# Loading the two halves of the first piece of x through ScalarE's queue in a gated attention and GLU kernel

## The chip, the cores and the metric

The kernel runs on one core of one Trainium2 chip. The metric is the time of one execution in device microseconds; the figure given for a kernel is the median of its runs. Below, TensorE (PE) multiplies matrices, PEld is its loading of the stationary operand, VectorE (DVE), ScalarE (ACT) and GpSimd (POOL) work on elements, and SyncE (SP) issues transfers. ScalarE can issue transfers too, from its own queue. A transfer is issued by an engine's queue and carried out by the core's 16 DMA engines; a semaphore tells when it has landed.

## The reference

The input x has 2048 rows of 512. The reference mixes two branches with a gate per row:

```
g = sigmoid(sum(x * gate_w))                      # one number per row
a = attention(x @ wqkv) @ wo                      # 32 heads of 16, each row sees the 256 rows up to itself
b = (sigmoid(x @ w_gate) * (x @ w_up)) @ w_down   # 1376 hidden columns
out = g * a + (1 - g) * b
```

All of it is float32.

## The kernel before

Every product of two float32 operands is made from three matmuls. An operand is split into a rounded high part, made by ScalarE's cast, and the rest, made by VectorE's subtraction (the function `split`, lines 75 and 76); the products high x high, high x low and low x high are added in PSUM. x is kept transposed in SBUF as `xh` and `xl`: 128 partitions, four pieces of the contraction (`d`, 0 to 3) and 2048 columns, which are the rows of x. It arrives in four chunks of 512 columns (`c`), each of four pieces `d` of 128 x 512.

The program runs in stages: the value projection of the first four blocks of 128 rows (tile `vps`, line 440), the query and key projections (`pj`), the rest of the value blocks, the windowed attention interleaved with the gate and up projections (`gu`), and last the down projection and the output projection (`pd`, `pa`). The order on TensorE, ScalarE, VectorE and SyncE is the order in which the program is written; a planner places only GpSimd's instructions. Waits on semaphores follow from the tiles that an instruction reads and writes. Eight semaphores serve the transfers in turn, so a transfer waits until the one eight before it has landed.

The change touches the first loads of the first stage. Before them line 185 issues 14 matmuls on zeros (`warm`). Then, for each `d`, the loop in lines 189 to 195 loads the value weights `wv` of that piece (256 KB), splits them into `wvh` and `wvl`, loads the piece of x of chunk 0 (256 KB) and splits it. For `d = 0` the piece of x is loaded and split in two halves of 256 columns (128 KB each), so that the matmuls of the first two blocks can begin with the first half. All these transfers are issued by SyncE. `xraw` and `wvraw`, into which they go, are parts of the tile `V`, which the profile therefore names as their destination; `wvh` goes by the name `w`. After the loop come the loads of the query and key weights (`wqraw`, line 144) and of the chunks 1 to 3 of x (line 168).

TensorE takes `d = 0` in two parts, the first two blocks for all three products and then the other two; from `d = 1` on it takes four blocks for each product:

```
for w, bb in (
    [(w, (2 * h, 2 * h + 1)) for h in range(2) for w in range(3)] if d == 0
    else [(w, range(4)) for w in range(3)] if d < ND - 1 else [(None, range(4))]
):
```

So `d = 0` has 12 matmuls, and those of its first half need `wv` piece 0 and the first half of x.

Of the kernel before, what the change touches and what calls it, by code (L numbers as in the profile page):

```python
# [22 lines left out]
CH = 512  # L23
# [33 lines left out]
def gated_mix_kernel(  # L57
# [11 lines left out]
    nc = tc.nc  # L69
# [4 lines left out]
    def split(hi, lo, src):  # L74
        nc.scalar.copy(hi, src)  # L75
        nc.vector.tensor_tensor(lo, src, hi.bitcast(F32), op=ALU.subtract)
# [52 lines left out]
    with ExitStack() as actx:  # L129
# [30 lines left out]
        xraw = Vf[:, NB * VROW - 2 * ND * CH:].rearrange("p (c d t) -> p c d t", c=2, d=ND)  # L160
# [22 lines left out]
        def idle_mm(n):  # L183
            for _ in range(n):
                mm(warm_ps[:, 0:2 * P], warm[:, 0:P], warm[:, 0:2 * P], start=True, stop=True)

        idle_mm(14)

        for d in range(ND):
            nc.sync.dma_start(wvraw[:, d], wv_v[:, d])  # L190
            split(wvh[:, d], wvl[:, d], wvraw[:, d])
            for h in range(2) if d == 0 else (None,):
                ts = slice(0, CH) if h is None else slice(h * CH // 2, (h + 1) * CH // 2)
                nc.sync.dma_start(xraw[:, 0, d, ts], xT[0, d][:, ts])
                split(xh[:, d, ts], xl[:, d, ts], xraw[:, 0, d, ts])
        raw_q = [load_wqk(g) for g in range(2)]
        load_x(1)
# [294 lines left out]
        def gu_mm(f, c, w, k, half=None, second=False):  # L492
            if (f, c, w) not in gp:
                gp[f, c, w] = ps.tile([P, CH], F32, tag="misc", name=f"gu{f}_{c}_{w}", bufs=3)
            group_mm(gp[f, c, w], gv[:, 0, w], gv[:, 1, w], c, k, half, second)
# [90 lines left out]
        def proj_slot(s, k, half):  # L586
            g, c = divmod(s, NC)
            d, w = divmod(k, 2) if k < 2 * ND else (k - 2 * ND, 2)
            r = slice(64 * half, 64 * half + 64)
            mm(pair_of_banks(f"ph{s}")[half], wq[g][int(w == 2)][r, d], (xl if w == 1 else xh)[r, d, c * CH:(c + 1) * CH],  # L590
               start=k == 0, stop=k == 3 * ND - 1)

        def proj_sum(s):
            lower, upper = halves.pop(f"ph{s}")
            t = cpool.tile([P, CH], F32, tag="sp", name=f"psum{s}", bufs=4)
            nc.scalar.copy(t, lower)
            pj[s] = t
            behind.append(lambda: nc.vector.tensor_tensor(t, upper, t, op=ALU.add))
            soon.append(lambda: proj_post(s))
# [6 lines left out]
                lambda k, h=None, x=False, a=(f, c, w): gu_mm(*a, k, h, x),  # L606
# [159 lines left out]
        for u in range(N):  # L766
# [34 lines left out]
            for s4 in proj_at.get(u, ()):  # L801
                if u < LAG:
                    first.insert(0, (
                        lambda k, h, s4=s4: proj_slot(s4, k, h), lambda s4=s4: proj_sum(s4)))
# [113 lines left out]
        for n, (c, f) in enumerate(steps):  # L918
# [34 lines left out]
            for t in range(4):  # L953
                ts = slice(t * P, (t + 1) * P)
# [72 lines left out]
```

## Time and profile before

| what | value |
|---|---|
| time, median of 3 runs | 738.04 us (737.7 to 738.16) |
| time of the profiled execution | 737.77 us |
| its span, first to last instruction | 736.1 us |
| TensorE busy | 730.0 us, 99% of the span |
| VectorE, ScalarE, GpSimd busy | 507.1, 430.4, 170.7 us |
| granted TensorE clock | 1.000 |
| moved by the DMA engines | 103.65 MB, mean 141 GB/s |

In a row of the view in order of time the first number is the start in us from the beginning of the span, the second the length; then come engine, line, operation, destination and source with their shapes and the count. Brackets hold the idle time ahead of it and what ended it. SPq is the queue in which SP issues transfers; the length there is that of the issue, not of the transfer. In the view of stretches each engine has its busy time and the number of its instructions, and the last three columns are the granted clock of TensorE, the busy share of the 16 DMA engines and the rate in GB/s. In the chain of work that ended last each row is start, length and what held the chain.

### The profile page before, as it was taken

How to read it: one execution, taken by the hardware profiler on the slowest of the kernel's cores; microseconds unless marked ns; L12 is line 12 of the kernel's file. 1: busy time of each engine (PE TensorE's matmuls, PEld its weight loads, DVE VectorE, ACT ScalarE, POOL GpSimd, SP SyncE). 2: the span in 40 equal slices, each digit the busy share in tenths (PEclk: the TensorE clock that was granted, in tenths of full speed). 3: DMA queues.
4: the chain of work that ended last, by engine and by line, in shares of the span. 5: the costliest groups of instructions: out<-in, count | busy, mean ns of one | idle time of the engine just before them, and what ended most of it. 6: DMA issues, size and time to landing. Idle time of an engine off the chain costs nothing.

```text
span 736.1 us, 17727 instructions
## 1 busy us (share of the span) xinstructions
PE 730.0 (99%) x6298; PEld 578.3 (79%) x6298; DVE 507.1 (69%) x1519; ACT 430.4 (58%) x922; POOL 170.7 (23%) x256
## 2 busy tenths in 40 slices
PE   9999999999999999999999999999999999999997
PEld 7888777887777878778777777778887888787886
DVE  5378867667776776776777677678846877658481
ACT  6423666576666666756757667676566654534341
POOL 5200333233233232323323323323341000000000
PEclk9999999999999999999999999999999999999999
DMA  8441334534445353452534524544477867878431
GB/s 300 108 116 43 102 106 120 152 88 127 129 116 142 86 153 109 123 156 59 165 106 107 152 76 128 160 135 152 154 233 190 281 173 175 224 172 252 131 74 57
DMA packets 94464, 103.65 MB, mean 141 GB/s; under 512 B 44942, under 2 KB 57486, under 8 KB 94376
## 3 DMA queue, kind: packets, MB, share of 16 engines
q1 hardware_dynamic: 94376, 102.53, 50.0%
q8 instruction: 49, 0.80, 0.5%
q14 instruction: 39, 0.32, 0.1%
HBM read 45.32 MB, written 31.99 MB: 105 GB/s over the span
## 4 chain that ended last, share of the span: by engine, by line
PE 97%; DVE 1%; DMA 1%; issue 1%; ACT 0%; SPq 0%; DVEq 0%
PE gu L245 28%; PE pv L394 12%; PE pj L245 11%; PE s L315 7%; PE st L361 5%; PE tp L539 5%; PE pd L79 5%; PE pd L81 5%; PE pd L80 5%; PE vh L576 3%; PE pa L79 2%; PE pa L80 2%; PE pa L81 2%; PE vps L440 1%; DVE junk L321 1%; DMA V<-in_wv_dram 1%
## 5 line engine op out<-in xcount | busy, mean ns | idle before, releaser
L321 DVE CUSTOM_DVE_ANT_0 junk<-s,mask 128x384 f32<-128x384 f32 (+2 forms) x512 | 271.6, 530 | 123.4 <-PE s L315 57.3
L366 ACT ACTIVATE pt<-st 128x384 f32<-128x384 f32 (+2 forms) x512 | 241.1, 475 | 166.0 <-PE st L361 66.6
L245 PE MATMUL gu<-xh,w 64*128 64x512 f32 x1152 | 271.1, 393 | 0.0
L245 PE MATMUL gu<-xl,w 64*128 64x512 f32 x576 | 183.0, 392 | 0.0
L371 POOL TENSOR_SCALAR_AFFINE_SELECT pt<-pt 128x512 f32<-128x512 f32 x128 | 86.5, 675 | 373.2 <-ACT pt L366 369.6
L361 PE MATMUL st<-ring 64*128 64x384 f32 (+2 forms) x536 | 168.1, 331 | 0.0
L315 PE MATMUL s<-ring 64*128 64x384 f32 (+2 forms) x536 | 166.7, 329 | 0.7 <-DVE mx L321 0.7
L245 PEld LDWEIGHTS gu<-xh,w 64*128 64x128 f32 x1152 | 150.9, 185 | 13.7
L315 PEld LDWEIGHTS s<-ring 64*128 64x128 f32 x536 | 95.3, 184 | 39.8 <-DVE nm L332 8.1
L361 PEld LDWEIGHTS st<-ring 64*128 64x128 f32 x536 | 96.3, 184 | 10.3 <-issue 2.7
L394 PE MATMUL pv<-pt,V 128*32 128x384 f32 (+2 forms) x1408 | 91.0, 388 | 0.0
L245 PEld LDWEIGHTS gu<-xl,w 64*128 64x128 f32 x576 | 87.7, 185 | 4.0
L245 PE MATMUL pj<-xl,wqh 64*128 64x512 f32 (+1 forms) x228 | 80.0, 392 | 0.0
L245 PE MATMUL pj<-xh,wqh 64*128 64x512 f32 (+1 forms) x228 | 79.8, 392 | 0.0
L376 POOL TENSOR_SCALAR_AFFINE_SELECT pt<-pt 128x512 f32<-128x512 f32 x112 | 74.8, 668 | 0.0
L245 PE MATMUL pj<-xh,wql 64*128 64x512 f32 (+1 forms) x228 | 69.8, 391 | 0.0
L394 PEld LDWEIGHTS pv<-pt,V 128*32 128x32 f32 x1408 | 37.2, 109 | 35.1 <-issue 28.8
L79 PE MATMUL pd<-ring,hb 128*128 128x512 f32 x160 | 63.1, 395 | 0.0
L81 PE MATMUL pd<-ring,hb 128*128 128x512 f32 x160 | 62.8, 393 | 0.0
L80 PE MATMUL pd<-ring,hb 128*128 128x512 f32 x160 | 62.1, 388 | 0.0
L75 ACT CAST hb<-V 128x512 fp32r<-128x512 f32 x40 | 24.9, 622 | 61.7 <-DVE V L730 47.7
L245 PEld LDWEIGHTS pj<-xh,wql 64*128 64x128 f32 (+1 forms) x228 | 41.2, 185 | 3.1
(129 smaller groups left out, 1133.1 us busy)
## 6 DMA issues: line engine op xcount, KB each, us to landing
gu_scratch<-sp SPq DMA_DIRECT2D x72, 256.0 KB
V<-gu_scratch SPq DMA_DIRECT2D x36, 512.0 KB
ring<-sh SPq DMA_DIRECT2D x128, 128.0 KB
ring<-sl SPq DMA_DIRECT2D x64, 128.0 KB
guraw<-in_wgu_dram SPq DMA_DIRECT2D x18, 256.0 KB
oT_scratch<-ob SPq DMA_DIRECT2D x128, 32.0 KB
xl<-oT_scratch SPq DMA_DIRECT2D x16, 256.0 KB
out_dram<-spare SPq DMA_DIRECT2D x16, 256.0 KB
```

What stands on the lines that cost most here:

```text
L79: mm(ps, lh, rh, start=first, stop=False)
L80: mm(ps, lh, rl, start=False, stop=False)
L81: mm(ps, ll, rh, start=False, stop=last)
L245: mm(pt, (wl if w == 2 else wh)[r, d], (xl if w == 1 else xh)[r, d, c * CH:(c + 1) * CH], start=k == 0 and not second, stop=k == 3 * ND - ...
L315: mm(pt[:, (k - k0) * P:(e - k0) * P], lhsT, blk(g, k, hh, 1, e - k), start=k == k0, stop=e == i + 1, skip_group_check=True,)
L321: nc.vector.tensor_tensor_reduce(junk[:, 0:n], pt[:, 0:n], mask[:, 3 * P - n:], scale=1.0, scalar=NEG, op0=ALU.add, op1=ALU.max, accum_out ...
L361: mm(pt[:, (q - j) * P:(e - j) * P], lhsT, blk(g, q, hh, 0, e - q), start=q == j, stop=e == last, skip_group_check=True,)
L366: nc.scalar.activation(pts[u][:, hh, 0:n], pt[:, 0:n], AF.Exp, scale=SCALE)
L371: nc.gpsimd.affine_select(p[:, :, 0:P], p[:, :, 0:P], pattern=[[0, HG], [1, P]], compare_op=ALU.is_ge, fill=0.0, base=0, channel_multiplie ...
L376: nc.gpsimd.affine_select(p[:, :, 2 * P:], p[:, :, 2 * P:], pattern=[[0, HG], [-1, P]], compare_op=ALU.is_gt, fill=0.0, base=0, channel_mu ...
L394: mm(pv[32 * hh:32 * hh + 32, (q % 4) * P:(q % 4 + e - q) * P], V[:, j, h * VW:h * VW + 32], p[:, hh, (q - j) * P:(e - j) * P], start=Fals ...
L539: mm(tp[b][:, 0:TW], (xl if w == 1 else xh)[r, d, b * P:(b + 1) * P], tw[d][int(w == 2)][r, 0:TW], start=k == 0 and not second, stop=k == ...
```

## The change

The two halves of the piece `d = 0` of x are issued by ScalarE, ahead of the loop. In the loop SyncE issues the four weight pieces and the pieces 1 to 3 of x. The splits, and the order of all that is computed, stay as they are.

```diff
         idle_mm(14)
 
+        pieces0 = [slice(h * CH // 2, (h + 1) * CH // 2) for h in range(2)]
+        for ts in pieces0:
+            nc.scalar.dma_start(xraw[:, 0, 0, ts], xT[0, 0][:, ts])
         for d in range(ND):
             nc.sync.dma_start(wvraw[:, d], wv_v[:, d])
             split(wvh[:, d], wvl[:, d], wvraw[:, d])
-            for h in range(2) if d == 0 else (None,):
-                ts = slice(0, CH) if h is None else slice(h * CH // 2, (h + 1) * CH // 2)
-                nc.sync.dma_start(xraw[:, 0, d, ts], xT[0, d][:, ts])
+            if d > 0:
+                nc.sync.dma_start(xraw[:, 0, d], xT[0, d])
+            for ts in pieces0 if d == 0 else (slice(0, CH),):
                 split(xh[:, d, ts], xl[:, d, ts], xraw[:, 0, d, ts])
         raw_q = [load_wqk(g) for g in range(2)]
```

## The prediction

> **What bounds the kernel now.** I read the page first: the share of each engine and the chain that ended last.
>
> ```profile
> span 736.1 us, 17727 instructions
> ...
> PE 730.0 (99%) x6298; PEld 578.3 (79%) x6298; DVE 507.1 (69%) x1519; ACT 430.4 (58%) x922; POOL 170.7 (23%) x256
> ...
> PE 97%; DVE 1%; DMA 1%; issue 1%; ACT 0%; SPq 0%; DVEq 0%
> ```
>
> TensorE is busy for 730.0 of 736.1 us and holds 97% of the chain. So this kernel is a single row of matmuls, and a change in how the first operands are loaded can pay only by what it moves at the start of that row. Everything behind the point from which TensorE no longer waits moves along by the same amount. The second view is therefore the chain in the first 9 us.
>
> ```profile
> 0.80 0.40 SPq L190
> ...
> 1.26 0.41 SPq L194
> ...
> 1.72 0.42 SPq L194
> ...
> 2.19 4.34 DMA V<-in_wv_dram
> ...
> 6.55 0.62 ACT w L75
> ...
> 7.19 0.63 ACT xh L75
> ...
> 7.86 1.19 PE vps L440 x4
> ```
>
> SP issues the first weight piece (I call it w0), the two halves of the first piece of x (x0a, x0b) and then the second weight piece (w1). w1 is on its way from 2.19 to 6.53 us. ScalarE rounds it, then rounds x1, and TensorE begins the second quarter of the contraction (d = 1) at 7.86. Three issues of SP stand ahead of w1 on this chain, and the change takes two of them away. The third view is ScalarE in order of time, to see when each operand is there.
>
> ```profile
> 0.80 1.28 ACT L75 ACT_TABLE_LOAD   x1 [0.80 <-PEq L1014]
> 3.54 0.62 ACT L75 CAST w<-V 128x512 fp32r<-128x512 f32 x1 [1.47 <-DMA V<-in_wv_dram]
> 4.07 0.40 ACT L75 CAST xh<-V 128x256 fp32r<-128x256 f32 x1
> 5.35 0.41 ACT L75 CAST xh<-V 128x256 fp32r<-128x256 f32 x1 [0.88 <-DMA V<-in_xT_dram]
> 6.55 0.62 ACT L75 CAST w<-V 128x512 fp32r<-128x512 f32 x1 [0.79 <-DMA V<-in_wv_dram]
> 7.19 0.62 ACT L75 CAST xh<-V 128x512 fp32r<-128x512 f32 x1
> ...
> 8.52 0.62 ACT L75 CAST xh<-V 128x512 fp32r<-128x512 f32 x1
> ```
>
> A cast begins 0.02 us after the transfer that it waited for (w1: 6.53 in the chain, 6.55 here). So w0 lands at 3.52, x0a by 4.07 (no wait ahead of its cast), x0b at 5.33, w1 at 6.53, x1 by 7.19. The fourth view is TensorE's weight loads, one for each matmul, in which a stop is seen more exactly than in the matmuls, whose ends are modelled.
>
> ```profile
> 4.52 0.49 PEld L440 LDWEIGHTS vps<-w,xh 128*128 128x128 f32 x2 [0.21 <-ACT xh L75]
> ...
> 6.90 0.42 PEld L440 LDWEIGHTS vps<-w,xl 128*128 128x128 f32 x2
> 7.86 0.76 PEld L440 LDWEIGHTS vps<-w,xh 128*128 128x128 f32 x4 [0.55 <-ACT xh L75]
> 8.67 0.87 PEld L440 LDWEIGHTS vps<-wvl,xh 128*128 128x128 f32 x4
> 9.59 0.89 PEld L440 LDWEIGHTS vps<-w,xl 128*128 128x128 f32 x4
> ```
>
> From 8.67 to 9.59 four loads take 0.92 us, 0.23 each. The twelve loads of d = 0 begin at 4.52; the last two begin at 6.90, so the first of d = 1 could follow at 6.90 + 2 x 0.23 = 7.36 and the fifth at 7.36 + 4 x 0.23 = 8.28. The fifth begins at 8.67. The stop before d = 1 costs 0.39 us, less than the 0.55 of idle shown, because loads run ahead of matmuls. After that the loads of this stage follow each other with no stop.
>
> **The change part by part.** *Two issues leave SP's queue.* These are the rows with the times of SP and the sizes.
>
> ```profile
> 0.80 0.40 SPq L190 DMA_DIRECT2D V<-in_wv_dram  x1
> 1.26 0.89 SPq L194 DMA_DIRECT2D V<-in_xT_dram  x2
> 2.19 0.43 SPq L190 DMA_DIRECT2D V<-in_wv_dram  x1
> ...
> 5.04 0.95 SPq L144 DMA_DIRECT2D wqraw<-in_wqk_dram  x2
> 6.55 1.64 SPq L168 DMA_DIRECT2D V<-in_xT_dram  x3
> ```
>
> ```profile
> V<-in_wv_dram SPq DMA_DIRECT2D x4, 256.0 KB
> V<-in_xT_dram SPq DMA_DIRECT2D x2, 128.0 KB
> ```
>
> w1 is issued at 1.26 in place of 2.19, 0.93 us earlier, and so is each piece after it, down to the loads of wqk at 5.04. The load at 6.55 waits for w1 to land (6.53); it is moved forward with w1. Nothing on TensorE waits for these later pieces, so they are costed at nothing: the cast of x2 ends at 9.14, and d = 2 begins 0.92 after the last group quoted, at 10.51. If that cover of 1.4 us were gone, a late piece would cost its own lateness and no more.
>
> *When w1 lands.* The fifth view is the transfers by stretch.
>
> ```profile
> 1.80:2.50 0.70, 0.70 (x6) 0.70 (x5) 0.00 (x0) 0.28 (x1) 0.66 (x3) 1.00 0.59 152
> 2.50:3.00 0.50, 0.50 (x4) 0.50 (x4) 0.00 (x0) 0.00 (x0) 0.44 (x2) 1.00 1.00 375
> 3.00:3.70 0.70, 0.70 (x5) 0.70 (x5) 0.00 (x0) 0.15 (x1) 0.68 (x1) 1.00 0.87 214
> 3.70:4.50 0.80, 0.80 (x5) 0.61 (x3) 0.30 (x1) 0.77 (x2) 0.00 (x0) 1.00 0.25 56
> ...
> 5.00:10.00 5.00, 4.89 (x21) 3.68 (x21) 3.33 (x7) 3.51 (x6) 0.00 (x0) 1.00 1.03 386
> ```
>
> The last three columns are the granted clock, the busy share of the 16 DMA engines and GB/s. The engines run at 386 GB/s once they have full-size pieces, but fall to 56 GB/s at 3.70 to 4.50, when only the halves of x were ahead of them. With w1 issued at 1.26 that hole is filled. By bytes: 106 KB up to 2.50 and 187 KB up to 3.00 as before, then 386 GB/s; w0, x0a, x0b and w1 are 786 KB (in thousands of bytes), moved by 3.00 + (786 - 293) / 386 = 4.28. Landing follows the last byte by about 0.6 us (w0's 262 KB are moved by 2.50 + (262 - 106) / 375 = 2.92 and it lands at 3.52). So w1 lands at about 4.9, an estimate; the ends are 3.98 (1.26 plus the 2.72 us that w0 took from issue to landing) and 5.60 (6.53 less 0.93). At each end the stop before d = 1 is gone: ScalarE casts w0, x0a, x0b, w1, x1 in 0.62 + 0.33 + 0.41 + 0.64 + 0.64 us, and with w1 at 5.60 ends x1 at 6.90, ahead of the 7.36 of before. What is late next is the first operand itself, w0.
>
> *Two issues enter ScalarE's queue.* No row shows an issue there. The nearest is SP's, 0.41 to 0.45 us each; the ends are none, and 1.28, the longest thing that this queue does at the start (its table load). I take SP's 0.45: two of them, 0.80 to 1.70, the table load from 1.70 to 2.98, still ahead of the first cast at 3.54. So the ScalarE side hides under the wait for w0. At 1.28 each the table load would end at 0.80 + 3 x 1.28 = 4.64, the first cast and TensorE 1.1 late, and the sum +0.7; that end belongs to the rivals. POOL's queue is not passed. If the table load goes first, x0a is issued at 2.08; that is a rival below.
>
> *w0 shares the engines with x0a.* Before, x0a was queued behind w0. Now both are there from 0.80 on. At 2.50 to 3.00 the engines are full (1.00), so what they move for x before the end of w0 puts off w0. Ends: none (x0a fits into the idle 41% of 1.80 to 2.50, 0.29 us of engine time) and 131 KB / 386 = 0.34 us (it all goes ahead of w0's end). I take 0.2, a little over the middle, because the idle share is nearly, but not quite, what x0a needs and comes as small pieces. The first matmul follows w0's landing by 1.00 us (3.52 to 4.52), since the casts of w0 and x0a lie between, and x0a has until 4.07 + 0.2 to land. TensorE therefore starts at 4.72. [...] No row here shows two queues at work.
>
> TensorE can take the earlier operand only when its warm-up matmuls are through:
>
> ```profile
> 3.76 0.84 PE L185 MATMUL warm_ps<-warm 128*128 128x256 f32 x3
> ```
>
> They end at 4.60, so a start much ahead of 4.52 isn't to be had, and the start at 4.72 leaves a hole of 0.1 us.
>
> *Sum.* Start of the row of matmuls +0.20, stop before d = 1 -0.39: **-0.19 us**, ends -0.39 and -0.05. The profiled execution took 737.77 us with 736.1 of span; it becomes 737.58. It lies 0.27 under the median of 738.04, inside the spread of the runs (737.7 to 738.16), so on the median I forecast 737.85.
>
> **The rivals.** *The change does nothing or a little harm by sharing.* If both halves go ahead of w0's end, w0 is 2 x 0.34 = 0.68 late, and the sum is 0.68 - 0.39 = +0.29: 738.33. For it: 1 KB rows kept the engines 0.87 busy for 214 GB/s at 3.00 to 3.70, so they are dear. Against it: x0b is issued 0.45 after x0a.
>
> *ScalarE's issues stand behind its table load, shared fairly.* x0a is issued at 2.08, moves from about 3.1 (w0's first bytes came within the stretch from 1.80, 1.0 after its issue), takes turns with w1: 131 + 262 KB at 386 is 1.02 us, so 4.1, landing 4.7, cast 0.43, start of TensorE 5.18: +0.66 - 0.39 = +0.27, 738.31. For it: the load stands at 0.80 now, the moment that the queue opens. Against it: it stands in front of the first cast, and the issues come ahead of that cast in the new order.
>
> *Slower, on the other side: x0a is served behind SP's backlog.* Same late issue, but the engines first move all that SP has queued by 2.5: w0, w1, x1, w2, 1049 KB. x0a is through at 3.00 + (1049 + 131 - 293) / 386 = 5.30, lands at 5.9, TensorE starts at 6.36: +1.84 - 0.39 = +1.45. With x2 ahead too it is 0.68 more, +2.1. I set this case at 739.9. It decides when x0a lands later than 5.9 us. For it: SP issues 256 KB every 0.47 us, faster than 386 GB/s move them, so a backlog there is. Against it: nothing shows one queue favoured.
>
> [...]
>
> *Faster by more.* The start can give no more than 0.39, so over 1.48 us would have to come from later stages, the stretch that VectorE paces:
>
> ```profile
> 62.00:72.00 10.00, 9.95 (x84) 8.66 (x82) 9.05 (x31) 4.36 (x10) 0.00 (x0) 1.00 0.10 24
> ```
>
> VectorE is busy 9.05 of 10 us; if it came in with 1.3 us less in arrears, the end would move by -0.39 - 1.3 = -1.7: 736.3. Against it: its work follows TensorE's, so it moves with it.
>
> **How the numbers follow.** Forecast 0.44 (737.6 to 738.1); sharing 0.19 (738.1 to 738.4); table load first, or issues as dear as it, 0.14 (738.1 to 738.8); backlog 0.17 (739.5 to 740.6); faster 0.06. 0.2% is 1.48 us, about what a measurement of this kernel can tell from no change. Faster is the last case, 0.06; slower is the backlog, 0.17; the other three lie within, 0.77. The range leaves out the faster case and the upper part of the backlog, some 0.1: 737.0 to 739.8; the low end is the bound of -0.39 on the lowest run and 0.3 for what the runs differ by.
>
> **What would show it.** SP issues w1 at about 1.26 and a second queue has rows; two issues on ScalarE before its table load; w0's cast at 3.5 to 3.9; weight loads from 4.5 to 4.9, with no stop at the start of d = 1; the span 0.0 to 0.4 shorter. A cast of x0a waiting for its transfer until 4.7 speaks for the table load first, until 5.9 for the backlog; a first cast at 4.2 for full sharing. The prediction is wrong if an issue on ScalarE takes over 1 us, if the new queue starts its transfers much later than SP's, or if the later stages don't move with the start.

## The result and the profile after

The changed kernel took 739.33 us in the median of 21 runs (737.41 to 740.13), the kernel before 737.92 (737.31 to 738.37, 21 runs); the ratio is 1.0013, with an interval of 1.0007 to 1.0019. So it became slower by about 1 us (0.5 to 1.4 by the interval), where 0.19 us less was forecast. The median alone misleads: the 21 times fall into two groups, ten from 737.41 to 738.29 and eleven from 739.33 to 740.13, and the kernel before has no such groups. In a second comparison (e1 below) five of eleven times lay in the upper group. The profiled execution, 739.99 us, is one of the upper group. Beside e5 to e8 two of 35 runs of the kernel before took 741.72 and 747.30 us at a granted clock of 0.958 and 0.949; all other runs, the upper group too, have a clock of 0.999 or 1.000.

The page of the changed kernel, with the added queue (q10) in its third part:

```profile
span 738.3 us, 17727 instructions
...
PE 732.0 (99%) x6298; PEld 579.4 (78%) x6298; DVE 506.8 (69%) x1519; ACT 430.2 (58%) x922; POOL 170.9 (23%) x256
...
q10 hardware_dynamic: 288, 0.26, 0.1%
...
PE 97%; DVE 1%; issue 1%; DMA 0%; ACT 0%; DVEq 0%
```

The span is 2.2 us longer, and 2.0 of that is TensorE's busy time, with the same 6298 matmuls. So in this execution most of the loss is matmuls that took longer, and not waits. Next, ScalarE and SP in order of time:

```profile
0.80 0.90 ACTq L191 DMA_DIRECT2D V<-in_xT_dram  x2
1.73 1.28 ACT L75 ACT_TABLE_LOAD   x1 [1.73 <-PEq L1017]
4.23 0.62 ACT L75 CAST w<-V 128x512 fp32r<-128x512 f32 x1 [1.21 <-DMA V<-in_wv_dram]
4.75 0.40 ACT L75 CAST xh<-V 128x256 fp32r<-128x256 f32 x1
5.36 0.41 ACT L75 CAST xh<-V 128x256 fp32r<-128x256 f32 x1 [0.21 <-DMA V<-in_xT_dram]
5.67 0.61 ACT L75 CAST w<-V 128x512 fp32r<-128x512 f32 x1
6.19 0.62 ACT L75 CAST xh<-V 128x512 fp32r<-128x512 f32 x1
```

```profile
0.80 0.87 SPq L193 DMA_DIRECT2D V<-in_wv_dram  x2
```

The two issues take 0.45 us each and stand ahead of the table load, and SP issues w1 right behind w0, as forecast. ScalarE no longer waits for w1 (its cast at 5.67 has no brackets). But w0 lands at 4.20 in place of 3.52. The transfers by stretch (granted clock, busy share, GB/s at the end of each row) show why:

```profile
1.80:2.50 0.70, 0.70 (x6) 0.70 (x5) 0.00 (x0) 0.70 (x1) 0.66 (x3) 1.00 0.83 208
2.50:3.00 0.50, 0.50 (x4) 0.50 (x4) 0.00 (x0) 0.50 (x1) 0.44 (x2) 1.00 0.88 221
3.00:3.70 0.70, 0.70 (x5) 0.70 (x5) 0.00 (x0) 0.02 (x1) 0.68 (x1) 1.00 1.01 294
3.70:4.50 0.80, 0.80 (x5) 0.61 (x3) 0.00 (x0) 0.27 (x1) 0.00 (x0) 1.00 1.01 370
```

The gap in the transfers at 3.70 to 4.50 is filled (370 GB/s, before 56). Up to 3.00, though, 0.70 x 208 + 0.50 x 221 = 256 KB were moved, less than the 293 before, and now w0, x0a and x0b share them: by 3.00 SP's queue had moved 0.19 MB and ScalarE's 0.07, where before all of the 0.29 MB came through SP's queue, w0 first. The last view is TensorE's matmuls in order of time; a row x2 holds two matmuls, so from its start to that of the next row it is two matmuls:

```profile
1.25 3.36 PE L185 MATMUL warm_ps<-warm 128*128 128x256 f32 x14 [1.25 <-DVE warm L180]
5.21 1.22 PE L443 MATMUL vps<-w,xh 128*128 128x512 f32 x2 [0.60 <-ACT xh L75]
6.23 1.05 PE L443 MATMUL vps<-wvl,xh 128*128 128x512 f32 x2
7.08 1.05 PE L443 MATMUL vps<-w,xl 128*128 128x512 f32 x2
7.93 1.05 PE L443 MATMUL vps<-w,xh 128*128 128x512 f32 x2
8.79 1.05 PE L443 MATMUL vps<-wvl,xh 128*128 128x512 f32 x2
9.64 1.05 PE L443 MATMUL vps<-w,xl 128*128 128x512 f32 x2
10.49 1.22 PE L443 MATMUL vps<-w,xh 128*128 128x512 f32 x4
11.55 1.09 PE L443 MATMUL vps<-wvl,xh 128*128 128x512 f32 x4
```

TensorE has nothing to do for 0.60 us ahead of its first real matmul. From 6.23 to 10.49 two matmuls take 0.85 us, 0.427 each, where the kernel before needed 0.23. From 10.9 on they take 0.23. The first twelve ran at half the rate. The sum up to the fifth weight load of d = 1, 8.67 before and 11.32 here:

```profile
1.25 3.06 PEld L185 LDWEIGHTS warm_ps<-warm 128*128 128x128 f32 x14 [1.25 <-DVE warm L180]
5.20 0.50 PEld L443 LDWEIGHTS vps<-w,xh 128*128 128x128 f32 x2 [0.89 <-ACT xh L75]
...
10.07 1.21 PEld L443 LDWEIGHTS vps<-w,xh 128*128 128x128 f32 x4
11.32 0.65 PEld L443 LDWEIGHTS vps<-wvl,xh 128*128 128x128 f32 x3
```

Start +0.68 (5.20 for 4.52); the stop ahead of d = 1 gone, -0.39; twelve loads in 4.87 in place of 2.84, +2.03; the first four of d = 1 in 1.25 in place of 0.92, +0.33. Together +2.65, as the rows show. The last matmul of the kernel starts at 734.17 in place of 731.76, so 2.41 of it is still there at the end of the row of matmuls; the span is 2.2 longer.

### The profile page after: what moved, and what is told of

The parts are those of the page before. It is cut to its first block, busy times and chain, and to the rows that moved or that the text cites. A ratio compares the mean times of both kernels' runs of the same rounds, so it can differ in the third digit from the quotient of the medians.

```text
span 738.3 us, 17727 instructions
## 1 busy us (share of the span) xinstructions
PE 732.0 (99%) x6298; PEld 579.4 (78%) x6298; DVE 506.8 (69%) x1519; ACT 430.2 (58%) x922; POOL 170.9 (23%) x256
## 4 chain that ended last, share of the span: by engine, by line
PE 97%; DVE 1%; issue 1%; DMA 0%; ACT 0%; DVEq 0%
PE gu L248 28%; PE pv L397 12%; PE pj L248 12%; PE s L318 7%; PE st L364 5%; PE tp L542 5%; PE pd L79 5%; PE pd L81 5%; PE pd L80 5%; PE vh L579 3%; PE pa L79 2%; PE pa L81 2%; PE pa L80 2%; PE vps L443 2%; DVE junk L324 1%
```

## The experiments

I call the time in which TensorE has no work between the last warm-up matmul and the first real one the hole. Theory A: the hole ahead of the first real matmul keeps TensorE at half rate for some microseconds more. Theory B: only the transfers differ between the two groups. Theory C: a second queue costs time by being used. Besides the time of each kernel, I read from each trace where the matmuls double their rate.

**e1: the changed kernel again.** No edit.

> The changed kernel once more, for a second trace of it: its times fall into two groups, about 737.4 to 738.3 and 739.3 to 740.1 us. In the trace of the upper group (739.99 us) w0 lands at 4.20, TensorE has nothing to do from 4.61 to 5.20, and its first twelve matmuls then start every 0.427 us in place of every 0.23. Theory A (the hole ahead of the first real matmul keeps TensorE at the lower rate): an execution of the lower group has its first twelve matmuls at 0.23 apart, or the slow ones end much sooner; the two groups differ by up to 12 x 0.197 = 2.4 us. Theory B (only the transfers differ between the groups): in an execution of the lower group w0 lands some 2 us earlier, or w1 and x1 do, and the matmuls of both groups have the same spacing. Median between 737.5 and 739.5 by both.

Measured: 737.98 us in the median of 11 runs, six from 737.46 to 737.98 and five from 739.28 to 740.12; ratio 1.0012 (1.0002 to 1.0021). The profiled execution is of the lower group, 737.76. ScalarE and the weight loads:

```profile
4.47 0.62 ACT L75 CAST w<-V 128x512 fp32r<-128x512 f32 x1 [1.46 <-DMA V<-in_wv_dram]
```

```profile
5.44 0.30 PEld L443 LDWEIGHTS vps<-w,xh 128*128 128x128 f32 x2 [1.13 <-ACT xh L75]
5.87 0.35 PEld L443 LDWEIGHTS vps<-wvl,xh 128*128 128x128 f32 x2
6.26 0.42 PEld L443 LDWEIGHTS vps<-w,xl 128*128 128x128 f32 x2
```

In this faster execution w0 comes even later (cast at 4.47) and TensorE starts at 5.44, but its matmuls are at the higher rate from the start (0.43 us and less for the first pairs, 0.46 for two from 6.26 on). Theory B falls: it is not the transfers that part the groups.

**e2: the changed kernel with 20 warm-up matmuls.**

```diff
-        idle_mm(14)
+        idle_mm(20)
```

> The changed kernel with 20 warm-up matmuls in place of 14, so that TensorE has work until about 5.5 us (14 take 1.25 to 4.6, 0.213 each) and no hole is left when w0 comes at 4.2. Theory A: the upper group disappears; the first real matmuls are 0.23 apart; the start at 5.2 to 5.5 costs at most 5.5 - 4.52 - 0.39 = +0.6 us against the kernel before, and if the warm-up turns to the higher rate on the way it is through sooner: 737.6 to 738.5. Theory B: both groups stay, and the upper one is at 739.3 to 740.4.

Measured: 738.54 us (737.75 to 739.43, 11 runs), ratio 1.0008 (0.9999 to 1.0017); ten of the eleven lie at or below 738.82, the last is 739.43. The weight loads of the traced execution:

```profile
1.25 4.34 PEld L185 LDWEIGHTS warm_ps<-warm 128*128 128x128 f32 x20 [1.25 <-DVE warm L180]
5.47 0.54 PEld L443 LDWEIGHTS vps<-w,xh 128*128 128x128 f32 x2
6.10 0.42 PEld L443 LDWEIGHTS vps<-wvl,xh 128*128 128x128 f32 x2
```

Of the upper group one time of eleven is left, and from the second real matmul (6.10) on the rate is the higher one, as theory A has it. 20 may be too many, since here they put off the second pair of loads to 6.10; the interval doesn't tell that from no loss.

**e3: the kernel before with 11 warm-up matmuls.** The same line with 11, in the kernel before; no transfer is touched.

> The kernel before, its transfers untouched, with 11 warm-up matmuls in place of 14: TensorE has nothing to do from about 3.97 until the first real matmul at 4.52, a hole of 0.55 us such as the change makes. Theory A: the times split into the same two groups, or move as a whole to the upper one, 739.5 to 740.5 in the upper. Theory B: nothing changes, 737.9 within 0.3, since no operand comes later.

Measured: 739.61 us (738.61 to 740.02, 10 runs), ratio 1.0019 (1.0010 to 1.0028). Six of the ten lie at 739.55 or more, one at 739.02, three at 738.6, and of 32 runs of the kernel before in that comparison none is over 738.72. Weight loads:

```profile
4.59 0.50 PEld L440 LDWEIGHTS vps<-w,xh 128*128 128x128 f32 x2 [0.92 <-ACT xh L75]
5.19 0.76 PEld L440 LDWEIGHTS vps<-wvl,xh 128*128 128x128 f32 x2
6.04 0.76 PEld L440 LDWEIGHTS vps<-w,xl 128*128 128x128 f32 x2
6.89 0.76 PEld L440 LDWEIGHTS vps<-w,xh 128*128 128x128 f32 x2
7.75 0.50 PEld L440 LDWEIGHTS vps<-wvl,xh 128*128 128x128 f32 x2
```

The traced execution is the fastest of the ten, 738.61. TensorE starts nearly as early as before (4.59) and still loses time: two loads are 0.85 apart until 7.75. A hole of 0.62 us alone, with one queue, made the loss. This is the direct test of theory A, and it brings the slowdown into the kernel before.

**e4: only x0b on ScalarE, behind a small copy.**

```diff
+        first = cpool.tile([P, 1], F32, name="first")
+        nc.scalar.copy(first, warm[:, 0:1].bitcast(F32))
         for d in range(ND):
             nc.sync.dma_start(wvraw[:, d], wv_v[:, d])
+            if d == 0:
+                nc.scalar.dma_start(xraw[:, 0, 0, pieces0[1]], xT[0, 0][:, pieces0[1]])
             split(wvh[:, d], wvl[:, d], wvraw[:, d])
-            for h in range(2) if d == 0 else (None,):
...
+            ts = slice(0, CH) if d else pieces0[0]
+            nc.sync.dma_start(xraw[:, 0, d, ts], xT[0, d][:, ts])
```

> Only the second half of the first piece of x is issued by ScalarE, behind one small copy, which brings the table load ahead of the issue; w0 and the first half stay with SP in the old order. All is computed as before. By the working of the prediction: w0 lands at 3.5 and x0a by 4.07 as before, so TensorE starts at 4.5 with no hole; w1 is issued at 1.72 in place of 2.19, lands at 5.6 to 6.1, and the stop of 0.39 us ahead of d = 1 shrinks to 0 or 0.2: 737.5 to 737.9, by theory A in one group. If an issue waits until the table load is through, it stands at about 2.1; if not, at about 0.9. Theory C (a second queue costs time by itself, wherever it stands): 739 or more, or two groups.

Measured: 738.15 us (737.81 to 739.09), ratio 1.0006 (0.9997 to 1.0015). ScalarE's rows:

```profile
0.80 1.28 ACT L190 ACT_TABLE_LOAD   x1 [0.80 <-PEq L1019]
1.24 0.39 ACTq L195 DMA_DIRECT2D V<-in_xT_dram  x1
2.09 0.19 ACT L190 COPY first<-warm 128x1 f32<-128x1 f32 x1
3.63 0.62 ACT L75 CAST w<-V 128x512 fp32r<-128x512 f32 x1 [1.35 <-DMA V<-in_wv_dram]
```

Here the issue behind the table load did not wait for it: it was made at 1.24, while the load ran to 2.08. With that the second queue is in use, w0 lands at 3.61, 0.09 later than before, and the time is that of the kernel before within the interval. So theory C falls as I had put it (739 or more, or two groups); a cost below the upper end of the interval, 1.1 us, isn't ruled out. TensorE started at 4.76, since x0a was cast only at 4.30 (4.07 before), and the stop ahead of d = 1 was gone, but no gain can be measured.

**e5: the changed kernel with 17 warm-up matmuls.** The line of e2 with 17.

> The changed kernel with 17 warm-up matmuls: the last one is through at about 5.04 us, where the array takes the next one, so that of the hole ahead of the first real matmul (5.2 to 5.45) at most 0.4 us is left, and nothing is put off as with 20 (which let the first real matmul start at 6.10 only). Theory A: the upper group is gone or rare, and what is left of the change is w0's lateness less the stop, +0.68 to +0.93 - 0.39 = +0.3 to +0.5: 738.2 to 738.5, under the 738.54 of 20. Rival (a hole of 0.2 to 0.4 us is already too long): two groups again, the upper one at 739.3 to 740.1.

Measured: 737.96 us (737.33 to 738.54, 12 runs), ratio 0.9997 (0.9988 to 1.0006): one group, the upper one gone, and with it the whole loss. That is less than the 738.2 to 738.5 that I had expected. In the traced execution, one of its slower ones (738.49), w0 came at 4.89:

```profile
1.25 3.35 PEld L185 LDWEIGHTS warm_ps<-warm 128*128 128x128 f32 x17 [1.25 <-DVE warm L180]
5.89 0.30 PEld L443 LDWEIGHTS vps<-w,xh 128*128 128x128 f32 x2 [1.28 <-ACT xh L75]
6.31 0.34 PEld L443 LDWEIGHTS vps<-wvl,xh 128*128 128x128 f32 x2
6.69 0.42 PEld L443 LDWEIGHTS vps<-w,xl 128*128 128x128 f32 x2
```

Its 17 loads take 3.35, hardly more than the 3.06 of 14: the last of them already ran at the higher rate (three more loads in 0.29 us, where at 0.213 they take 0.64), and the second real pair of loads follows the first by 0.42 us, in spite of the hole of 1.08 us ahead of them. Here the rate, once doubled, was still so behind the hole.

**e6: both halves on ScalarE, behind a small copy.**

```diff
+        first = cpool.tile([P, 1], F32, name="first")
+        nc.scalar.copy(first, warm[:, 0:1].bitcast(F32))
         pieces0 = [slice(h * CH // 2, (h + 1) * CH // 2) for h in range(2)]
```

> The changed kernel with one small copy on ScalarE ahead of the two issues. In the trace with only the second half on ScalarE this put the issue at 1.24 in place of 0.80. So x0a and x0b are issued at about 1.24 and 1.70, 0.44 behind w0. If w0 is late because both halves move beside it from its first byte on (the rival of the prediction with full sharing), it lands at 3.6 to 3.9 in place of 4.20 and 4.45, TensorE starts at 4.6 to 4.9, the hole is 0 to 0.3, and the time is 737.6 to 738.2 in one group, or nearly. If w0 is late because a second queue slows the transfers at the start whenever it is used, w0 stays at 4.2 or more and the two groups stay.

Measured: 738.95 us (738.08 to 740.80, 12 runs), ratio 1.0013 (1.0003 to 1.0024), with times from 738.1 to 739.1 and four from 740.0 to 740.8.

```profile
3.56 0.62 ACT L75 CAST w<-V 128x512 fp32r<-128x512 f32 x1 [1.28 <-DMA V<-in_wv_dram]
4.55 0.40 ACT L75 CAST xh<-V 128x256 fp32r<-128x256 f32 x1 [0.37 <-DMA V<-in_xT_dram]
```

Issued 0.44 us later, the halves no longer hold up w0 (3.54, before 3.52). So its lateness in the changed kernel (4.20) comes from sharing the engines from its first bytes on. But now x0a, issued at 1.24 beside w1, is late (4.53), and a hole of 0.40 us ahead of TensorE's start stays. My expectation for the time was wrong in that: I had followed w0 alone.

**e7: e4 with 15 warm-up matmuls.** The line of e2 with 15.

> Only the second half on ScalarE behind a small copy, with 15 warm-up matmuls in place of 14. That kernel's trace with 14 had no stop ahead of d = 1 any more, but a hole of 0.15 us ahead of the first real matmul (4.61 to 4.76) and two and a half matmuls at 0.43 to 0.59 apart before the rate doubled, about 0.5 us. Theory A: with the hole filled this is had back in part: 737.6 to 738.0, 0.1 to 0.4 under the 738.15 with 14. Rival (the moment of the doubling has nothing to do with so short a hole): 738.1 to 738.3, unchanged.

Measured: 738.19 us (737.93 to 739.17), ratio 1.0000 (0.9991 to 1.0009); unchanged against e4 by these intervals, so the expected 0.1 to 0.4 was not had. In the traced execution x0a was cast only at 4.70 and a hole of 0.34 us stayed, so that a filled hole was not tried.

**e8: one queue, w1 ahead of x0b.**

```diff
         for d in range(ND):
-            nc.sync.dma_start(wvraw[:, d], wv_v[:, d])
+            if d != 1:
+                nc.sync.dma_start(wvraw[:, d], wv_v[:, d])
...
+                if h == 1:
+                    nc.sync.dma_start(wvraw[:, 1], wv_v[:, 1])
```

> SP issues all as before, with one order changed: the second weight piece (w1) ahead of the second half of x. w0 and x0a are untouched, so TensorE starts at 4.52 with no hole; w1 is issued at 1.72 in place of 2.19 and lands at 4.9 to 5.6, x0b at 5.3 to 5.9 (its cast is needed by 5.97). If what the change could win is only the place of w1 in the queue, it is won here without a second queue: no stop ahead of d = 1, -0.2 to -0.39: 737.55 to 737.75. Rival (x0b comes later than 5.6 and stops TensorE in d = 0): 737.9 to 738.3.

Measured: 738.24 us (737.86 to 738.75), ratio 0.9992 (0.9971 to 1.0013), with 738.07 for the kernel before: the rival came true. x0b was cast at 6.56 and the weight loads stood for 1.23 us in the middle of d = 0:

```profile
6.56 0.40 ACT L75 CAST xh<-V 128x256 fp32r<-128x256 f32 x1 [2.04 <-DMA V<-in_xT_dram]
```

```profile
7.01 0.30 PEld L443 LDWEIGHTS vps<-w,xh 128*128 128x128 f32 x2 [1.23 <-ACT xh L75]
```

**e9 and e10: the kernel before with 12 and with 17 warm-up matmuls.** The same line with 12 and 17.

> The kernel before with 12 warm-up matmuls in place of 14, transfers untouched: the hole ahead of the first real matmul is about 0.3 us (with 11 it was 0.62, with 14 none). Theory A: a hole of this size still costs in part of the executions; median between 738.1 and 739.6, the highest at 739.3 or more. If only holes over about 0.5 us matter: 737.9 to 738.1, none above 738.7.

> The kernel before with 17 warm-up matmuls, the control for the changed kernel with 17: there is no hole in either, and the transfers differ. If the warm-up is at the lower rate to its end, the first real matmul starts at 5.2 to 5.3 in place of 4.52, and with the stop of 0.39 hidden behind that the time is +0.3: 738.2 to 738.4; if the rate doubles on the way, less. Were w0's lateness worth 0.3 to 0.5 us, the changed kernel with 17 (737.96) should have come out slower than this one; by the reading that the lateness beyond the stop is worth next to nothing, both lie within 0.4 of each other.

Measured: with 12, 738.10 us (737.66 to 738.45), ratio 1.0001 (0.9993 to 1.0010); with 17, 738.01 us (737.58 to 738.92), ratio 1.0004 (0.9995 to 1.0013). A hole of 0.31 us doesn't show in the times, so theory A in the form that I had given it there falls: this short hole cost nothing that these runs can tell. (In the traced execution of e9 six matmuls ran at half rate all the same, since the rate doubled only at 7.44; the kernel before may have such late doublings too, by its spread of 1 us.) And 737.96 (e5) against 738.01 (e10) says that w0's lateness less the stop is worth nothing that these runs can tell.

**e11: only x0a on ScalarE.**

```diff
-        for ts in pieces0:
-            nc.scalar.dma_start(xraw[:, 0, 0, ts], xT[0, 0][:, ts])
+        nc.scalar.dma_start(xraw[:, 0, 0, pieces0[0]], xT[0, 0][:, pieces0[0]])
...
-            if d > 0:
-                nc.sync.dma_start(xraw[:, 0, d], xT[0, d])
+            ts = slice(0, CH) if d else pieces0[1]
+            nc.sync.dma_start(xraw[:, 0, d, ts], xT[0, d][:, ts])
```

> Only the first half of the first piece of x is issued by ScalarE, at 0.80 beside w0; the second half stays with SP, behind w0 and ahead of w1. By sharing from the first byte on, w0 is late by half of what two halves made it: 3.52 + 0.34 to 0.47 = 3.85 to 4.0 (with both: 4.20, 4.28, 4.45, 4.89); TensorE starts at 4.85 to 5.0, the hole is 0.25 to 0.4, and part of the executions are in the upper group: median 737.7 to 739. If w0's lateness comes from a second queue being in use at all, w0 stays at 4.2 or more. If the order of the issues alone counts, w0 lands at 3.5.

Measured: 738.07 us (737.44 to 740.17, 11 runs), ratio 1.0006 (0.9997 to 1.0015); three of eleven from 739.52 up.

```profile
3.98 0.62 ACT L75 CAST w<-V 128x512 fp32r<-128x512 f32 x1 [1.46 <-DMA V<-in_wv_dram]
```

w0 lands at 3.96, 0.44 late: one half costs about half of what two cost (0.68, 0.76, 0.93 and 1.37 in four traces). The upper group is rarer but not gone.

**All traces together.** Besides the views, each trace holds records of the granted clock. The first one begins where the spacing of the matmuls shows that the rate doubles; ahead of it there is no record, and the column shows 1.00 all the same. "Idle" is TensorE's time without work from the last warm-up matmul to the first real one.

```
kernel               warm-up  idle us  rate doubles at us  time of that execution
before                 14      0            4.95             737.77
after                  14      0.60        10.77             739.99
e1  (after)            14      0.84         4.54             737.76
e2  (after)            20      0            6.08             738.25
e5  (after)            17      1.08         4.13             738.49
e11 (x0a alone)        14      0.35         7.07             738.43
e6  (both, behind)     14      0.40         6.26             738.77
e4  (x0b alone)        14      0.15         5.81             738.34
e7  (x0b alone)        15      0.34         4.71             738.31
e8  (one queue)        14      0.13         4.11             738.10
e3  (before)           11      0.62         7.90             738.61
e9  (before)           12      0.31         7.44             738.38
e10 (before)           17      0            4.32             737.58
```

The rate doubled anywhere from 4.11 to 10.77 us, and the traces part by whether that was ahead of the hole. In four it was (e1, e5, e7 and e8, with holes of 0.84, 1.08, 0.34 and 0.13 us), and there the second real pair of loads follows the first by 0.34 to 0.43 us. In six it was not, and there the second pair follows by 0.59 or 0.60, and the doubling came behind the first real load by 1.05 (e4, hole 0.15), 1.26 (e6, 0.40), 2.11 (e11, 0.35), 2.95 (e9, 0.31), 3.31 (e3, 0.62) and 5.57 us (the changed kernel, 0.60). In the three without a hole it came 0.43 (before) and 0.61 us (e2) behind the first real load, and ahead of it in e10. That fits the two groups: the trace of the lower one (e1) doubled ahead of its hole, that of the upper one behind it. It is a reading of thirteen traces, not a test; why the rate doubles when it does, and from what length on a hole puts that off, they don't show. Why half of the changed kernel's 32 executions fell on each side is left open. So are the upper times of e11 (three of eleven) and e6 (four of twelve): the holes of their traced executions, 0.35 and 0.40 us, are shorter than the 0.60 of the changed kernel's, and no execution from their upper times was traced.

## Why the prediction was wrong

- *The bound, and what carries over.* Right: TensorE is one row of work, and a shift at its start is still there at matmuls far behind (+2.65 at the fifth load of d = 1, +2.41 at the last matmul).
- *Two issues leave SP's queue.* Right for w1: issued at 1.26, landed at 5.14 (4.9 was forecast), no wait for it, no stop ahead of d = 1, in both traces of the changed kernel. Wrong for "each piece after it": the ninth transfer, x3, waits for the semaphore of the first, which is now x0a (landed at 4.40), and is issued at 4.41, only 0.16 us earlier than before, and the loads of wqk at 4.78 for 5.04. TensorE waited for none of them.
- *Two issues on ScalarE.* Right: 0.45 us each, ahead of the table load, hidden. The rival of the table load first is answered by e4: the issue was made at 1.24, while the load ran to 2.08.
- *w0 shares the engines with x0a.* Mis-sized: I took +0.2 with 0.34 as the upper end; it measured +0.68 and +0.93. The rival with both halves ahead of w0's end gave 0.68. I had counted on the idle share of 1.80 to 2.50 to carry x0a for nothing; that stretch did move more (208 GB/s for 152), but the bytes moved by 3.00 fell from 293 to 256 KB. The 0.34 was also short, as it counted x0a alone, and at the full 386 GB/s: with x0a alone on the second queue (e11) w0 was 0.44 late. How two queues share the engines was an assumption of mine; of the order in which they are served, no run here shows more than these landings and bytes.
- *"The start at 4.72 leaves a hole of 0.1 us."* This is the step that failed. The hole was 0.60 and 0.84 by the size just told, and I had priced a hole at its own length. What a hole does to the rate of the matmuls behind it stood in the sum at nothing. In the trace of the upper group the twelve loads of d = 0 took 4.87 us in place of 2.84, +2.03; by the times about half of the executions are of this group. The evidence was in the profile of before: the warm-up matmuls of 256 columns were 0.213 us apart, the real ones of 512 columns 0.23, so the warm-up ran at about half the rate. I read the clock column, 1.00, and asked nothing more of it.
- *The backlog on SP's queue*, the only case that I gave for slower, didn't occur; its chance of 0.17 belonged to the clock, which I hadn't listed. That 739.33 lies inside my 737.0 to 739.8 is luck: the upper part of that range stood for the backlog.
- *The time.* +1.0 by the ratio, where -0.19 was forecast; within the 0.2% of no change, to which I had given 0.77, but on the other side.

## What to carry to other kernels

Warm-up work should leave no long hole ahead of the first real operand, in any execution, as long as the rate has not doubled (0.31 us cost nothing that could be measured here, 0.6 us did); a change that makes the first operand later needs its warm-up lengthened with it (14 to 17 here took away the whole loss). Here a second queue brought no bandwidth up to 3.00 us (256 KB for 293): what it issued beside the first operand came out of the first operand's time, so issue ahead only what is needed first. And where the median jumps between two values, look at all times and trace one execution of each group.

## What the runs showed of the hardware that was not expected

- The clock column shows 1.00 where the trace has no clock record, and TensorE at that time ran at half rate (0.213 us for 256 columns, then 0.427 for 512; behind the doubling 0.23 for 512). The spacing of like matmuls is the safer reading.
- The doubling came anywhere from 4.11 to 10.77 us in thirteen traces. In the changed kernel's trace it came 5.57 us behind the first real load, with a hole of 0.60 us ahead of that load; in e5's it had come at 4.13, and the rate behind a hole of 1.08 us was the higher one.
- An issue on ScalarE's queue was made at 1.24 while its table load ran from 0.80 to 2.08, though it stood behind it in order.
- The second half of x, in 1 KB rows on SP's queue, landed between 5.33 and 5.92 us when issued at 1.72; issued by ScalarE at 1.24 (e4) it was there when the cast of the first half was through: both were cast in one go from 4.30 on. What slows it on the one queue was not tried.
